# A new order for a three-layer kernel: gap memsets as operations of their own, gate loads charged more, late loads searched together

## The chip, the core and the metric

The kernel runs on one core of a Trainium2 chip. The core has a matrix engine (PE, with its weight loads shown apart as PEld), a vector engine (DVE), an activation engine (ACT), a general engine (POOL) and an engine that only issues transfers (SP); sixteen DMA engines move data between DRAM and the core's SBUF. The metric is the device time of one execution in microseconds, lower is better.

## What is computed

Windowed attention (64 keys back, 4 batches, 8 heads, 576 positions), then a gated two-matrix layer with a token shift, then a layer in which a five-tap convolution gates a product before the last one:

```python
scores = q @ k.T / sqrt(64); scores = where(0 <= i - j < 64, scores, -1e9)
x = softmax(scores) @ v                               # (4, 576, 512)
xk = mu_k * x + (1 - mu_k) * x_prev; xr = mu_r * x + (1 - mu_r) * x_prev
x = sigmoid(xr @ w_r) * (relu(xk @ w_k) ** 2 @ w_v)   # 512 -> 1024 -> 512
gate = sigmoid(sum(conv_w[k] * xpad[:, k:k + S, :] for k in range(5)))
out = (gate * (x @ w_val)) @ w_out
```

Everything is float32. Products are kept near that precision by splitting each operand into a rounded high part and a low rest and adding three products (high by high, high by low, low by high).

## The kernel before

**Stages.** The 2304 positions (4 batches of S = 576 in a row) go through attention and the first layer in five blocks t of 256, 512, 512, 512 and 512 positions. Attention works in 20 units of one block and one pair of heads. `qk` computes scores, `top`, `exp`, `eps`, `rec` and `norm` are the softmax, `tr` transposes the weights, `pv` is the product with the values, `x` puts the result in place; `ldqk` and `ldv` load a unit. The first layer has products `r`, `h` and `v` (PE, line 724, 512 columns each; line 748 for block 0), whose inputs are mixed by `a` and `xm` and split by `xhi` and `xlo`. Its weights come in as `w_r`, `w_k` and `w_v` in pieces (`ld`), which DVE and ACT turn from 64-bit to 32-bit floats. Block t's result goes to a DRAM buffer x2d (`st t m`, shown as x2d<-sgs).

The second layer works by batch b. `ldx b` loads the batch from x2d into a tile xb (1152 KB, line 868; xb<-x2d). `xsum`, `xhi_` and `xlo_` make its operands, in seven pieces by Strassen's scheme. Each of the seven products `val b m1` to `m7` is 12 matmuls of 288 columns (line 1006). They share two PSUM banks, u and v. Bank u's running sum is copied off by `valu` (ACT, early<-val), and `valc` (DVE, lines 1047 and 1052) adds up and empties a bank before the next product may start in it. `gv` multiplies by the gate, `gsum`, `ghi_` and `glo_` make operands again, and `out b m1` to `m7` are the last products with copies `outu` (ACT, ou<-out). For the first three batches `o` copies a part of the output to st and `os` stores it; then `oa` on POOL adds the rest from the same ou buffers into DRAM by an accumulating transfer (out_t<-ou). An ou buffer is free again when that has landed. Batch 3 takes plain products, `out 3`.

**Gate.** For batches 0 to 2 the convolution is done early, while PE is on the first layer, in six tasks n: `cld n` loads half a batch from x2d (576 KB, line 924), `ctap n f k` are ten taps (the first on ACT, four on DVE at line 937, for two halves f), `cgate n` the sigmoid (ACT, line 941), `cst n` the store to a DRAM buffer gd (576 KB, gd<-early). `cld n` waits for the taps of n - 1, and the first tap of n for `cst n-1`. `ldg b` brings the gate back (gate<-gd). Batch 3's gate is computed late (`tap`, `part`, `acc`).

**Second weights.** They are turned and stored to DRAM during the first layer, and come back when its matrices are no longer needed: `wv2` (wk<-w_val, 1792 KB, two) and `wo2` (wr<-w_out and wol<-w_out, 1024 KB, four). The first product with them, `out 0 m1`, waits for all four `wo2`.

**Order.** Nothing is scheduled while the kernel runs. A table SLOT gives each operation of each kind a place in one overall order, and with a letter the engine where there is a choice (v DVE, a ACT, p POOL). `Plan.run` walks that order and emits each operation, so every engine, and SP's queue of transfers, executes its own operations in the table's order and waits at each for what it needs. The durations and the `moves` in the calls of `op` serve the search that made the table; besides, `run` uses them to place a few filler matmuls on PE in the first 15 us. Two operations emit more than their own engine's instruction: `ldx` has a POOL memset of the four-column gap ahead of its transfer (line 867, batch 3 only), `cld 0` one on line 923. At the start, `first` (POOL) zeroes a column of xT; `cap` makes a mask: a DVE memset (line 337), then four POOL selects; `eye` and `low` on DVE turn it and an identity into matmul operands for the first `qk`.

The line that the last stage hangs on most: `turn_s` frees the first layer's memory for the tiles of odd batches, so `ldx 1` can't start before the last `v` product has read its weights.

Of the kernel before, what the change touches and what calls it, by code (L numbers as in the profile page):

```python
# [27 lines left out]
NF = DM // P  # L28
# [15 lines left out]
    'first': '39',  # L44
    'warm': '4',
    'cap': '8',
    'ident': '6',
    'band': '243',
    'low': '9',
    'eye': '7',  # L50
    'table': '11',
    'ldmu': '1',
    'ldc': '430',
    'mu': '2',
    'omu': '26',
    'pg': '62',
    'wc0': '439 432 460',
    'wc': '461',
    'first_x': '27',
    'ldqk': '3 13 15 16 17 37 122 166 231 255 276 277 305 327 409 434 443 467 491 540',  # L60
    'ldv': '23 36 47 49 132 140 219 224 237 261 340 363 369 415 469 482 495 550 581 584',
    'qk': '10 14 18 30 43 72 128 183 252 264 278 314 338 389 410 435 453 490 513 542',
    'top': '12 19 24 33 52 80 133 195 272 284 304 322 350 406 427 446 477 507 525 586',
    'exp': '20 21 28 41 61 95 149 197 287 292 312 323 359 416 428 458 484 520 563 592',
    'eps': 'v29 p22 p38 p51 p97 p162 p150 p215 v288 p298 v329 p332 p380 v421 p429 p474 p492 p554 v566 p593',
    'rec': '31 34 46 63 105 171 161 228 289 300 331 342 381 422 447 476 504 555 577 601',
    'diag': 'v32 v35 v58 v66',
    'tp': '40 48 64 73',
    'pt': 'v42 a55 v67 a93',
    'pv': '44 56 78 96 156 205 234 247 302 325 361 376 400 442 483 508 530 572 588 614',  # L70
    'x': 'v53 v65 a86 a100 a180 a208 a235 a249 v313 a330 a366 a383 a403 a448 a486 a509 a536 v573 v604 a647',
    'norm': 'v111 v176 v189 a232 v293 v301 v337 a357 v382 a423 v450 a493 v514 v556 a583 v609',
    'tr': '119 192 225 242 294 318 343 375 399 433 454 499 515 557 587 612',
    'mask': '262 270 297 319 344 395 412 437 471 500 517 558',
    'edge': '265 281 303 321 346 405 426 444',
    'a': 'a60 a71 a94 a102 a54 a68 a101 a103 a211 a226 a257 a260 v368 v371 v386 v392 a455 v472 a549 a551 '
        'v594 a610 a734 v748',
    'xm': '70 81 99 112 75 88 126 117 240 245 286 267 373 374 417 394 511 489 568 565 689 686 736 749',
    'xlo': '74 82 106 115 77 98 127 146 254 259 339 271 379 391 420 404 545 528 582 569 714 743 752 817',
    'carry': '177 230 285 328 402 473 535 595',  # L80
    'r': '84 109 116 123 85 92 114 131 89 110 118 124 87 90 121 138 351 360 356 370 516 512 529 533 651 688 '
        '698 727 835 827 844 855',
    'sig': '125 136 142 143 365 387 388 413 526 531 544 576 670 711 738 744 850 856 865 870',
    'h': '141 151 145 147 152 167 154 169 174 181 185 186 172 184 194 198 280 282 299 295 310 326 315 347 '
        '449 407 440 457 481 478 485 494 608 611 605 641 643 648 678 675 778 774 772 786 792 800 816 820',
    'relu': 'a159 a164 a175 a178 a193 a200 a199 a201 a290 a296 v311 a317 a341 v345 a348 a349 a451 v452 v441 '
        'v470 v497 v498 a521 a522 v627 v639 a629 a642 a659 a669 a683 a684 a787 a794 v791 a805 v818 v819 '
        'v828 a833',
    'sbuf': '165 179 204 206',
    'slo': 'v188 a182 v212 a207 336 335 354 364 496 503 538 532 658 682 697 702 812 826 852 851',  # L90
    'v': '213 216 221 239 248 253 258 269 390 424 367 385 414 456 398 419 564 574 548 559 561 570 578 580 '
        '737 741 742 756 746 750 732 733 893 902 863 892 859 867 884 891',
    'x2': '263 275 283 273 425 401 459 438 597 560 571 599 753 777 766 745 905 899 901 897',
    'st': '333 358 377 397 436 431 519 501 598 606 615 635 776 780 810 770 969 940 983 903',
    'xhi': 'a246 a251 v316 a268 a378 a384 v418 a396 v539 a527 v579 v567 a699 v735 a747 v767',
    'cut': '227 266 372 393 488 562',
    'shi': '308 320 352 355 466 475 505 523 646 649 680 685 807 808 822 834',
    'sq': 'v309 v324 v353 v362 v468 a480 a534 v524 v655 a679 a696 a701 v809 a815 a823 a845',
    'staging': '0',
    'w_r ld': '25 45',  # L100
    'w_r g': '50 79',
    'w_r t': '57 76',
    'w_r s': '59 83',
    'w_r hi': 'v139 v91',
    'w_r lo': '148 144',
    'w_k ld': '69 104 155 135',
    'w_k g': '107 129 160 153',
    'w_k t': '108 130 158 137',
    'w_k s': '120 134 173 168',
    'w_k hi': 'v191 a214 a196 a187',  # L110
    'w_k lo': '223 229 203 222',
    'w_v ld': '157 170 218 217',
    'w_v g': '163 190 233 241',
    'w_v t': '202 210 238 250',
    'w_v s': '209 220 244 256',
    'w_v hi': 'a279 a274 v408 v306',
    'w_v lo': '334 291 411 307',
    'wide_x': '236',
    'turn': '860',
    'turn_s': '915',  # L120
    'turn_w': '880 868',
    'w_val ld': '541 585 624 662',
    'w_val room': '589 628 633 663',
    'w_val g': '603 630 634 664',
    'w_val t': '600 617 618 621 619 607 632 644 637 645 625 638 665 660 674 666 677 707 692 708',
    'w_val s': '616 631 636 676',
    'w_val hi': 'a623 v656 a690 a709',
    'w_val lo': '626 661 694 716',
    'w_val st': '640 654 667 673 693 700 715 724',
    'w_out ld': '668 687 713 760',  # L130
    'w_out room': '695 717 754 782',
    'w_out g': '703 718 755 788',
    'w_out t': '691 705 706 710 726 720 722 757 764 762 739 773 783 775 789 796 811 821 813 825',
    'w_out s': '704 721 763 806',
    'w_out hi': 'v729 v768 a802 v829',
    'w_out lo': '730 781 804 837',
    'w_out st': '758 731 769 784 803 824 831 838',
    'wv2': '890 839',
    'wo2': '917 881 896 873',
    'ldx': '861 920 952 1004',  # L140
    'gbuf': '869 925 1025 1051',
    'ldg': '871 966 1077',
    'xhi_': 'a882 v878 v876 a886 a889 a906 a933 a971 a927 a937 a953 a961 a970 a1005 a994 a1002 a1026 a1028 '
        'a1087 v1127 a1075 a1098 a1143 a1117',
    'xlo_': '898 909 883 887 911 912 934 973 932 942 974 964 988 1078 1009 1011 1056 1038 1091 1138 1093 1113 '
        '1147 1136',
    'xsum': '866 879 885 888 923 930 945 955 980 993 1022 1027 1074 1081 1103 1115',
    'val': '904 908 918 921 924 929 936 939 944 946 959 976 986 992 998 1082 1019 1035 1043 1088 1062 1107 '
        '1100 1122 1133 1142 1155 1161',
    'valu': 'a910 a919 a926 a943 a963 a977 a1014 a1039 a1053 a1110 a1126 a1149',  # L150
    'valc': '913 931 935 941 951 985 990 1001 1083 1054 1101 1073 1123 1153 1174 1168',
    'gv': '914 938 949 947 999 1000 996 1017 1092 1114 1120 1086 1152 1179 1195 1170',
    'ghi_': 'v916 a948 a962 a957 a967 a982 a987 a1006 a1032 a1049 a1018 a1031 a1040 a1042 a1094 a1102 a1144 '
        'a1128 a1139 a1157 v1148',
    'glo_': '922 956 972 958 968 997 989 1033 1044 1050 1024 1036 1045 1046 1111 1116 1145 1129 1140 1158 1151',
    'gsum': '950 960 965 978 1015 1029 1034 1041 1121 1131 1137 1146',
    'out': '928 975 979 984 995 1012 1013 1037 1052 1060 1063 1068 1095 1089 1112 1125 1154 1134 1160 1166 '
        '1173 1177 1178 1186 1187 1198 1199 1200 1205',
    'outu': 'a954 a991 a1007 a1048 a1066 a1084 v1124 a1156 a1162',
    'o': '981 1010 1030 1021 1058 1085 1104 1090 1130 1163 1176 1182 1185 1193 1201 1203 1206',  # L160
    'os': '1003 1020 1071 1023 1079 1099 1164 1108 1180 1175 1181 1183 1192 1194 1202 1204 1208',
    'oa': '1008 1047 1065 1106 1135 1141 1189 1184 1188',
    'tap': '1055 1059 1069 1057 1067 1070 1064 1076 1080 1072 1097 1105',
    'part': '1016 1061 1109 1132',
    'acc': '1096 1118 1119 1167',
    'gate': '1150 1169',
    'ghi': 'v1159 v1171 v1196 v1190',
    'glo': '1165 1172 1197 1191',
    'oh': '1207',
    'cld': '445 546 650 751 801 849',  # L170
    'ctap': '462 464 479 487 502 463 465 506 510 518 575 590 591 596 613 547 552 553 602 620 653 671 719 723 '
        '728 657 672 681 712 725 761 785 790 793 797 765 771 779 795 798 832 840 841 842 843 830 836 846 '
# [1208 lines left out]
```

## Time and profile before

| | before |
|---|---|
| median of 3 runs | 412.71 us (411.44, 412.71, 413.06) |
| the profiled execution | 411.4 us |
| its span (first to last record) | 409.4 us |
| PE busy | 402.3 us, 98% of the span |
| PEld, DVE, ACT, POOL busy | 341.0, 344.7, 252.6, 27.9 us |
| granted TensorE clock | 1.00 of full speed throughout |

The span is what the trace covers; 2.0 us of the execution lie around it. A matmul is pipelined and its end is modelled, so PE counts as busy through part of a short wait: the distance from one matmul's start to the next tells more than the busy share. "Idle before" is a gap that the trace shows on an engine, with what ended it.

### The profile page before, as it was taken

How to read it: one execution, taken by the hardware profiler on the slowest of the kernel's cores; microseconds unless marked ns; L12 is line 12 of the kernel's file. 1: busy time of each engine (PE TensorE's matmuls, PEld its weight loads, DVE VectorE, ACT ScalarE, POOL GpSimd, SP SyncE). 2: the span in 40 equal slices, each digit the busy share in tenths (PEclk: the TensorE clock that was granted, in tenths of full speed). 3: DMA queues.
4: the chain of work that ended last, by engine and by line, in shares of the span. 5: the costliest groups of instructions: out<-in, count | busy, mean ns of one | idle time of the engine just before them, and what ended most of it. 6: DMA issues, size and time to landing. Idle time of an engine off the chain costs nothing.

```text
span 409.4 us, 10877 instructions
## 1 busy us (share of the span) xinstructions
PE 402.3 (98%) x4578; PEld 341.0 (83%) x4578; DVE 344.7 (84%) x516; ACT 252.6 (62%) x603; POOL 27.9 (7%) x74
## 2 busy tenths in 40 slices
PE   8999999999999999999999999999999899999996
PEld 4788887778787787788888888888889899999996
DVE  5999999999784779959979799979397699999960
ACT  5999988748435576947747643066322386866631
POOL 2001121010000000100000000000000001122010
PEclk9999999999999999999999999999999999999999
DMA  8999554050520634151378337465999906778666
GB/s 287 413 419 356 204 174 128 2 160 0 160 85 2 207 120 149 53 195 37 119 202 298 133 141 271 179 243 198 368 430 347 381 4 202 190 170 194 115 173 146
DMA packets 24673, 78.36 MB, mean 191 GB/s; under 512 B 3376, under 2 KB 6704, under 8 KB 21808
## 3 DMA queue, kind: packets, MB, share of 16 engines
q1 hardware_dynamic: 22608, 72.64, 49.3%
q0 software_dynamic: 1872, 5.01, 7.6%
q8 instruction: 36, 0.59, 0.6%
q14 instruction: 13, 0.11, 0.1%
q10 hardware_dynamic: 144, 0.00, 0.0%
HBM read 51.80 MB, written 23.49 MB: 184 GB/s over the span
## 4 chain that ended last, share of the span: by engine, by line
PE 85%; DVE 5%; DMA 5%; issue 2%; ACT 2%; POOL 0%; SPq 0%; ACTq 0%; POOLq 0%
PE h L724 22%; PE v L724 22%; PE r L724 11%; PE sv L636 5%; PE v L748 4%; PE h L748 3%; PE sv L590 3%; PE out L1118 3%; PE out2m L1006 3%; PE val3m L1006 3%; DMA xb<-x2d 2%; PE r L748 2%; DMA out_t<-ou 2%; DVE x L903 1%; PE out1m L1006 1%
## 5 line engine op out<-in xcount | busy, mean ns | idle before, releaser
L724 PE MATMUL h<-x,wk 128*128 128x512 f32 x384 | 91.3, 394 | 0.0
L724 PEld LDWEIGHTS h<-x,wk 128*128 128x128 f32 x384 | 71.2, 188 | 15.6
L724 PE MATMUL v<-sh,wv 128*128 128x512 f32 x256 | 81.3, 393 | 0.0
L724 PEld LDWEIGHTS v<-sh,wv 128*128 128x128 f32 x256 | 48.1, 188 | 10.6
L724 PE MATMUL v<-sl,wv 128*128 128x512 f32 x128 | 49.9, 390 | 0.0
L937 DVE SCALAR_TENSOR_TENSOR early<-early,wc 128x576 f32<-128x576 f32 x48 | 38.2, 810 | 12.2 <-ACT early L935 11.9
L724 PE MATMUL r<-x,wr 128*128 128x512 f32 x192 | 45.3, 391 | 0.0
L463 ACT ACTIVATE s<-s,m 128x96 f32<-128x96 f32 x104 | 37.2, 362 | 9.9 <-DVE m L452 9.9
L724 PEld LDWEIGHTS r<-x,wr 128*128 128x128 f32 x192 | 35.8, 188 | 7.6
L724 PEld LDWEIGHTS v<-sl,wv 128*128 128x128 f32 x128 | 24.1, 188 | 4.8
L776 ACT ACTIVATE rk<-h 128x512 f32<-128x512 f32 (+1 forms) x27 | 13.9, 543 | 20.6 <-PE h L724 19.0
L636 PEld LDWEIGHTS sv<-pt,vt 32*64 32x64 f32 x1536 | 18.8, 130 | 5.6 <-issue 3.1
L684 DVE SCALAR_TENSOR_TENSOR xm<-xT,omu,xm 128x512 f32<-128x512 f32 x32 | 22.4, 746 | 1.0 <-POOL xT L690 1.0
L707 DVE TENSOR_TENSOR x<-xm,x 128x1024 fp32r<-128x1024 f32 x16 | 19.5, 1220 | 3.0 <-ACT x L704 2.9
L800 ACT ACTIVATE sh<-rk 128x1024 fp32r<-128x1024 f32 x16 | 16.7, 1058 | 6.4 <-DVE rk L778 6.3
L636 PE MATMUL sv<-pt,vt 32*64 32x32 f32 (+2 forms) x1536 | 20.6, 238 | 0.0
L806 DVE TENSOR_TENSOR sl<-rk,sh 128x1024 fp32r<-128x1024 f32 x16 | 19.3, 1221 | 0.7 <-ACT rk L804 0.6
L463 ACT ACTIVATION_READ_ACCUMULATOR s<-s,m 128x1 f32 x104 | 19.8, 191 | 0.0
L830 DVE TENSOR_TENSOR sgs<-v,sgs 128x512 f32<-128x512 f32 (+1 forms) x20 | 12.3, 629 | 8.9 <-PE v L724 8.9
L935 ACT ACTIVATE early<-early,wc 128x576 f32<-128x576 f32 x12 | 8.8, 770 | 16.1 <-DMA gd<-early 10.9
L900 ACT ACTIVATE x<-xt 128x576 fp32r<-128x576 f32 x15 | 10.2, 678 | 9.9 <-DVE xt L893 9.9
L624 DVE STREAM_TRANSPOSE pt<-s 128x768 f32<-128x768 f32 x16 | 15.5, 968 | 0.4 <-ACT s L475 0.2
(226 smaller groups left out, 823.5 us busy)
## 6 DMA issues: line engine op xcount, KB each, us to landing
qk<-qk SPq DMA_DIRECT2D x16, 544.0 KB, 4.7
vt<-vh SPq DMA_DIRECT2D x16, 384.0 KB, 4.8
xb<-x2d SPq DMA_DIRECT2D x4, 1152.0 KB, 9.0
out_t<-st SPq DMA_DIRECT2D x15, 288.0 KB, 2.9
w_out<-w SPq DMA_DIRECT2D x8, 512.0 KB, 2.8
w_val<-w SPq DMA_DIRECT2D x8, 448.0 KB, 2.7
wk<-w_val SPq DMA_DIRECT2D x2, 1792.0 KB, 13.0
early<-x2d SPq DMA_DIRECT2D x6, 576.0 KB, 5.2
```

The costliest lines, as they stand in the source:

```text
L463: ACT.activation(out=s, in_=scores()[:, 2 * c // n_s, c % (n_s // 2), :] if scores else s, func=AF.Exp, scale=D ** -0.5 if scores else 1.0 ...
L624: V.transpose(out=a["pt"][:, :m2 * KW], in_=a["s"].rearrange("p c j -> p (c j)"))
L636: PE.matmul(a["o"][heads[h], i, j0 * HW:j1 * HW], lhsT=a["v"][r, k, heads[h]], rhs=p, start=k == 0, stop=k == m + 1, skip_group_check=True)
L684: V.scalar_tensor_tensor(out=m, in0=xT[:, f, :n], scalar=omu[:, c:c + 1], in1=m, op0=ALU.mult, op1=ALU.add)
L707: lambda E: E.tensor_tensor(out=dst(1), in0=src(), in1=f32(dst(0)), op=ALU.subtract))
L724: PE.matmul(ps, lhsT=a, rhs=b[:, kt, :], start=(kt == 0 and i == 0), stop=(kt == nk - 1 and i == 2))
L748: PE.matmul(Ps[key][:, :n], lhsT=ws(kt), rhs=x()[:, kt, :], start=kt == 0, stop=kt == nk - 1)
L776: ACT.activation(out=o, in_=ps, func=AF.Relu)
L800: ACT.activation(out=Ss[t][0][:, f, :n], in_=rk(), func=AF.Square)
L806: lambda E: E.tensor_tensor(out=Ss[t][1][:, f, :n], in0=rk(), in1=f32(Ss[t][0][:, f, :n]), op=ALU.subtract))
L937: V.scalar_tensor_tensor(out=o, in0=x, scalar=c, in1=o, op0=ALU.mult, op1=ALU.add)
L1006: PE.matmul(z[bank][:, j, :HS], lhsT=lhs, rhs=rhs, start=new and kt == 0 and e == 0, stop=kt == 1 and e == 2, skip_group_check=not new)
```

## The change

Three edits in the code that describes the work, and a new table. The memset of xb's gap becomes an operation `xbuf b` (on POOL for batch 3, nothing for the others), and the one of `cld 0` an operation `zero`; both stand in the order by themselves, and the transfers wait for them as before. In the costs that the search uses, a load and a store keep their duration, `moves` of `cld` goes from 1450 to 2100 and that of `ldx 3` from 4000 to 3300. Then nearly every row of SLOT has new numbers, and some operations a new engine. The work itself is the same: the same 3138 matmuls with the fillers among them, the same 149 transfers on SP's queue. After the table, the changed kernel's line numbers are 2 to 4 higher.

```diff
 SLOT = {
-    'first': '39',
-    'cap': '8',
+    'first': '0',
+    'cap': '5',
...
-    'ldx': '861 920 952 1004',
+    'xbuf': '837 922 949 1021',
+    'ldx': '849 923 964 1031',
...
+    'zero': '375',
...
     def load(b):
-        def go():
+        gap = GAP if b not in SPLIT else 0
+
+        def buffer():
             xb = Q["own", b % 2].tile([P, NF * (GAP + S)], F32, tag="xb", name=f"xb{b}")
-            gap = GAP if b not in SPLIT else 0
             Xb[b] = xb[:, :NF * (gap + S)].rearrange("p (f t) -> p f t", f=NF)
             if gap:
                 G.memset(Xb[b][:, :, 0:gap], 0.0)
-            DMA.dma_start(out=Xb[b][:, :, gap:], in_=x2d[:, b])
...
-        op(("ldx", b), "dma", 420, [("st", i, m) for i in t for m in range(NF)] + ["turn_s" if b % 2 else "turn", *last],
-           go, moves=4000 if b not in SPLIT else 2950)
+        op(("xbuf", b), "pool" if gap else "none", 120 if gap else 0, ["turn_s" if b % 2 else "turn", *last], buffer)
+        op(("ldx", b), "dma", 420, [("xbuf", b), *[("st", i, m) for i in t for m in range(NF)]],
+           lambda: DMA.dma_start(out=Xb[b][:, :, gap:], in_=x2d[:, b]), moves=3300 if gap else 2950)
...
-        def go():
-            if n == 0:
-                G.memset(cx[:, :, :GAP], 0.0)
-            DMA.dma_start(out=cx[:, :, GAP:], in_=x2d[:, b, fs])
-        op(("cld", n), "dma", 420, [("st", t, m) for t in ts for m in (2 * p, 2 * p + 1)] + old, go, moves=1450)
+        if n == 0:
+            op("zero", "pool", 120, old, lambda: G.memset(cx[:, :, :GAP], 0.0))
+            old = ["zero"]
+        op(("cld", n), "dma", 420, [("st", t, m) for t in ts for m in (2 * p, 2 * p + 1)] + old,
+           lambda: DMA.dma_start(out=cx[:, :, GAP:], in_=x2d[:, b, fs]), moves=2100)
```

Place 1, SP's queue between the second weights' first load and the load of the third batch. wk, wol and wr are second weights, gd<-early is `cst`, early<-x2d is `cld`, gate<-gd is `ldg`, x2d<-sgs is `st`; xb_3618, xb_3804 and xb_3928 are batches 0, 1 and 2 before, xb_3552, xb_3811 and xb_3906 the same ones now. Before:

```order
L1284 DMA wk_63<-w_val_106 128x3584
L1287 DMA wol_3661<-w_out_109 128x2048
L836 DMA x2d<-sgs 128x512
L943 DMA gd<-early 128x1152
L1287 DMA wr_65<-w_out_108 128x2048
L868 DMA xb_3804<-x2d 128x2304
L836 DMA x2d<-sgs 128x512
L868 DMA xb_3928<-x2d 128x2304
```

Now:

```order
L1290 DMA wr_66<-w_out_108 128x2048
L1290 DMA wol_3609<-w_out_109 128x2048
L956 DMA gate_3666<-gd 128x2304
L1290 DMA wr_65<-w_out_108 128x2048
L946 DMA gd<-early 128x1152
L1290 DMA wol_3605<-w_out_109 128x2048
L875 DMA xb_3811<-x2d 128x2304
L838 DMA x2d<-sgs 128x512
```

The big wk loads and batch 0's load stand earlier and are no longer in this stretch; the last `st` ahead of batch 1's load is now behind it; between the last `cst` and batch 1's load there is still one weight load of 1024 KB.

Place 2, ACT where batch 1's operands begin. The names early<-val0m are `valu 0`, x<-xb is `xhi_ 1 0` of batch 1, early<-early is `cgate 5`. Before:

```order
L941 ACTIVATE early<-early 128x1152
L900 ACTIVATE x<-xt 128x576
L1018 ACTIVATE early<-val0m_3742 128x576 x3
L900 ACTIVATE x<-xt 128x576
L900 ACTIVATE x<-xb_3804 128x1152
```

Now:

```order
L944 ACTIVATE early<-early 128x1152
L1021 ACTIVATE early<-val0m_3747 128x576
L903 ACTIVATE x<-xb_3811 128x1152
L1021 ACTIVATE early<-val0m_3747 128x576
L903 ACTIVATE x<-xt 128x576 x2
```

One of the three copies `valu 0` went to DVE, and the last of them stands behind an operation that waits for batch 1's load.

Place 3, ACT in the third batch's products of the first matrix. ou<-out1m are `outu 1`, st<-out1m are `o 1`, gate_4201 and gate_4211 with line 964 or 967 are `tap 3`, and sgs or tt at line 977 or 980 are `part 3`. Before:

```order
L1018 ACTIVATE ou<-out1m_4164 128x576
L900 ACTIVATE gq<-gate_3833 128x576
L1018 ACTIVATE early<-val2m_4065 128x576
L964 ACTIVATE gate_4201<-xb_4083,wc 128x576 x2
L1086 ACTIVATE st<-out1m_4202 128x576
L977 ACTIVATE sgs<-xb_4083,wc 128x576 x2
L964 ACTIVATE gate_4201<-xb_4083,wc 128x576
L1018 ACTIVATE ou<-out1m_4164 128x576
```

Now:

```order
L903 ACTIVATE gq<-gt 128x576 x2
L1021 ACTIVATE early<-val2m_4093 128x576
L1021 ACTIVATE ou<-out1m_4174 128x576
L967 ACTIVATE gate_4211<-xb_4125,wc 128x576 x2
L980 ACTIVATE tt<-xb_4125,wc 128x576 x2
L1021 ACTIVATE ou<-out1m_4174 128x576
L1089 ACTIVATE st<-out1m_4214 128x576
```

Between the first and the second `outu 1`, which empties bank u for a product of batch 1, ACT had eight operations, five of them of batch 3's gate; now it has four, all of batch 3's gate. On PE, `out 0 m3` now runs two products earlier (ahead of `val 2 m1` and `out 0 m4`, not behind `out 0 m4`), and `out 1 m7` one product earlier (ahead of `out 1 m5`). At the start, DVE's memset of `cap` is now ahead of the two casts that wait for POOL's identity, and in the first block's loads `ldv 4` stands behind two `w_k` pieces and an `ldqk`.

## Rows read from the trace of the kernel before

**Rows 1.** Page, part 1: busy us, share of the span, instructions.
```profile
PE 402.3 (98%) x4578; PEld 341.0 (83%) x4578; DVE 344.7 (84%) x516; ACT 252.6 (62%) x603; POOL 27.9 (7%) x74
```

**Rows 2.** Busy time by stretch, by engine; then clock, DMA share, GB/s.
```profile
20.00:30.00 10.00, 10.00 (x124) 8.13 (x123) 9.96 (x18) 9.95 (x29) 0.00 (x0) 1.00 1.01 415
...
310.00:320.00 10.00, 10.00 (x71) 9.65 (x70) 5.87 (x9) 1.31 (x2) 0.00 (x0) 1.00 0.98 339
320.00:330.00 10.00, 8.75 (x64) 8.31 (x63) 8.53 (x12) 3.99 (x6) 0.00 (x0) 1.00 0.70 290
...
360.00:370.00 10.00, 9.33 (x70) 9.09 (x69) 9.32 (x14) 6.02 (x10) 2.60 (x3) 1.00 0.81 172
```

**Rows 3.** PE timeline: start us, us, instruction, [idle before, what ended it].
```profile
321.54 1.76 PE L1006 MATMUL val0m<-x,wk 128*128 128x288 f32 x12
323.71 1.86 PE L1006 MATMUL val0m<-x,wk 128*128 128x288 f32 x12 [0.41 <-DVE early L1047]
326.41 0.77 PE L1006 MATMUL val1m<-x,wk 128*128 128x288 f32 x4 [0.83 <-DVE gate L1052]
...
361.54 0.29 PE L1006 MATMUL out1m<-gq,wol 128*128 128x288 f32 x1
362.51 0.54 PE L1006 MATMUL out1m<-gq,wr 128*128 128x288 f32 x2 [0.67 <-ACT ou L1018]
```

**Rows 4.** Chain that ended last, in time: start us, us, what.
```profile
290.35 21.77 PE v L724 x96
...
312.14 9.28 DMA xb<-x2d
...
331.60 1.34 DVE gq L903 x2
...
354.42 7.30 DMA out_t<-ou
...
373.97 1.60 PE out2m L1006 x12
...
404.37 1.61 PE last L1118 x12
```

**Rows 5.** DMA issues of 308.5 to 309.3 us: size, us to landing.
```profile
wr<-w_out SPq DMA_DIRECT2D x1, 1024.0 KB, 9.7
gd<-early SPq DMA_DIRECT2D x1, 576.0 KB, 5.4
```

**Rows 6.** The same, issues of 312.1 to 312.4 us.
```profile
xb<-x2d SPq DMA_DIRECT2D x1, 1152.0 KB, 9.3
```

**Rows 7.** The same, issues of 337.9 to 338.4 us.
```profile
xb<-x2d SPq DMA_DIRECT2D x1, 1152.0 KB, 5.7
```

**Rows 8.** Timelines of DVE and ACT, 283 to 322 us.
```profile
283.81 3.26 DVE L937 SCALAR_TENSOR_TENSOR early<-early,wc 128x576 f32<-128x576 f32 x4
...
307.40 1.17 ACT L941 ACTIVATE early<-early 128x1152 f32<-128x1152 f32 x1 [2.23 <-DVE early L937]
...
321.44 0.76 DVE L893 TENSOR_TENSOR xt<-xb 128x576 f32<-128x576 f32 x1 [3.21 <-DMA xb<-x2d]
```

**Rows 9.** Timelines of ACT and POOL, 349 to 355 us.
```profile
349.07 0.65 ACT L1086 ACTIVATE st<-out0m 128x576 f32<-128x576 f32 x1 [0.60 <-PE out0m L1006]
...
354.42 0.86 POOL L1091 DMA_DIRECT2D out_t<-ou  x1 [4.85 <-DMA out_t<-st]
```

**Rows 10.** Timeline of the first 8 us.
```profile
2.12 0.17 DVE L337 MEMSET cap<- 128x128 f32 x1
...
6.57 0.42 PEld L527 LDWEIGHTS s<-early 64*64 64x64 f32 x16 [0.20 <-DMA early<-qk]
...
7.30 0.69 DVE L454 TENSOR_REDUCE first_m<-s 128x4 f32<-128x512 f32 x1 [0.20 <-PE s L527]
```

**Rows 11.** DMA issues of 22.0 to 22.5 us, then PE timeline.
```profile
x<-w_k SPq DMA_DIRECT2D x1, 1024.0 KB, 10.3
...
33.43 1.28 PE L636 MATMUL sv<-pt,vt 32*64 32x32 f32 x96
```

260 rows, old and new, of the table SLOT are left out of this document.

## Prediction

> **What bounds the kernel now.** The first view is the busy time of the engines: PE holds 402.3 of 409.4 us, 98%, and no other engine comes near in a way that could set the end (PEld overlaps PE, DVE is at 84%) [rows 1]. So only time in which PE does not run can be won or lost, and the share hides where that is. The second view, busy time by stretch at a clock of 1.00 throughout, shows it: the stretch 20 to 30 and the stretch 310 to 320 are full, 320 to 330 has 8.75 us and 360 to 370 has 9.33 [rows 2]. The third is the PE timeline. I read starts, not shown idle, because the end of a matmul is modelled: one product of twelve matmuls takes 1.60 us [rows 4], one matmul 0.13 (1.60/12). The product that starts at 321.54 should be followed at 323.14 and is followed at 323.71, 0.57 late; the next comes at 326.41, 1.10 late; and the matmul after 361.54 comes at 362.51, 0.84 late [rows 3]. That is 2.5 us in three stalls. The rest of the span outside the start and the last transfer is one matmul after the other, so an order that only shuffles work there is worth nothing.
>
> The chain that ended last says the same from the other side: last `v` product from 290.35 for 21.77 us, then 9.28 us of batch 1's load, and later 7.30 us of an accumulating store; nearly all else on it is PE [rows 4].
>
> **Batch 1's load (stalls one and two).** It may be issued when the last `v` product has read its weights, at 312.1 (290.35 + 21.77), and lands 9.3 us later [rows 4, 6]. DVE has nothing else and idles 3.21 us until 321.44 [rows 8]; then it owes `xsum`, `xlo_` and the two `valc` on which PE waits, named in [rows 3] as L1047 and L1052. Why 9.3? The third batch-sized load of this kind takes 5.7 us with the queue free [rows 7]. Here a store of 576 KB and a weight load of 1024 KB, issued at 308.5 to 309.3, land 5.4 and 9.7 us later, so at about 314 and 318.5 to 319 [rows 5], and batch 1's 1152 KB follow 2.5 to 3 us behind, about what they cost at 415 GB/s (1.18 MB/415 = 2.8 us) [rows 2]. The load was not slow, it stood in line.
>
> The new order leaves the same two transfers directly ahead of it, takes the 256 KB `st` away from the head (0.6 us at 415 GB/s), and issues batch 0's load and a 1792 KB weight load earlier, in front of a load of gate data, so the backlog is worked off sooner. The last gate store hangs on eight taps of DVE (two groups of four at 3.26 us [rows 8]) and a sigmoid of 1.17 us [rows 8]. They now start from a batch 0 that is there earlier; I put the sigmoid's end at about 307 to 307.5 instead of 308.6 (307.40 + 1.17). What then lies ahead of batch 1's load at 312.1 is the end of one 1024 KB load. The lower bound of its landing is 312.1 + 5.7 = 317.8, the upper one today's 321.4. I take **318.5**: nearer to the free queue, because the two ahead are 1.6 MB, 4 us at 415 GB/s, and have over four us from 307.5 to 312.1.
>
> What PE needs: the order of its products is the same up to `val 1 m1`, so without stalls the last two `val 0` start at 321.54 and 323.14 and `val 1 m1` at 324.74. DVE is done with batch 0's first gate product at about 318.9 (before: its last operation of that kind ends some 3.21 before 321.44, at 318.2 [rows 8]; the new order gives it one copy from ACT, 0.7). From then, or from the landing if later, it does two `xsum`, one `xlo_` of double size and the first `valc`, five single operations of 0.67 (1.34 for two [rows 4]), 3.35 us, so the bank is free at 322.3, in time for 323.14. Two more `xlo_` and the second `valc` end at 324.3, in time for 324.74. On ACT a new danger stands: one `valu` is now behind batch 1's double `xhi_`, 1.15 us by the sigmoid's 1.17 for the same size [rows 8], plus 0.65 for itself, as a copy of the same size in [rows 9]. Landing plus 1.8 must stay under 321.54. Both hold for a landing up to about 319.4. Then stalls one and two are gone: **-1.67 us** (0.57 + 1.10). At a landing of 320 some 0.6 comes back; at today's 321.4 the `valu` costs 1.7 and the second `valc` 0.4, together 2.1, more than today's 1.67 by 0.4.
>
> **The accumulating store (stall three).** `out 1 m7` waits for the copy that empties bank u, and that copy for room in the staging tile, which the accumulating store on POOL holds: issued at 354.42, 7.30 to land [rows 4, 9], so 361.7. POOL waited 4.85 us for the plain store of the same rows [rows 9], which began with ACT's copy at 349.07, straight behind PE's `out 0 m3` [rows 9]. In the new order `out 0 m3` is two products earlier (3.2 us), and 1.67 more by the stalls gone: the accumulating store lands at 361.7 - 4.9 = 356.8. `out 1 m7` itself is one product earlier: 361.67 - 1.60 - 1.67 = 358.4. The copy of 0.65 then ends at 357.5, or at 358.2 if ACT's four gate operations in front (some 0.7 each, an estimate from that copy) come last. **-0.84 us**, with a margin of only 0.2; the other end is 0.
>
> **The start.** The memset of `cap` at 2.12 [rows 10] moves ahead of two casts and the mask is ready up to half a microsecond earlier. But the scores wait for a load until 6.57, and the softmax's first reduction follows PE at 7.30 [rows 10]; both stay. 0, ends -0.5 and +0.3. **The first block's loads.** `ldv 4` goes behind two `w_k` pieces and one `ldqk`. These are 1024 KB each, 10.3 us from issue to landing for the one issued at 22.0 to 22.5 [rows 11], hence 32.3 to 32.8, and `pv 4` reads its values at 33.43 [rows 11]. 0, ends 0 and +1.0. **The memsets as operations** sit on POOL, busy 7% [rows 1], ahead of transfers that wait for other things anyway; 0, at most one small memset (0.17 as [rows 10]) if POOL were late. The new charges of the gate loads exist in the search alone: 0.
>
> **The sum.** -1.67 - 0.84 = -2.5, so 411.4 becomes 408.9. The profiled execution was 1.3 below the median of the runs (412.71); the forecast for a median is 408.9 + 1.3 = **410.2**. A difference under 0.5%, 2.1 us, can hardly be told from none here; 2.5 is just over.
>
> **Rivals.** (A) *Batch 1's load stays late.* If transfers in flight shared the engines, instead of coming one behind the other, batch 1's load would share with batch 2's load and the gate load issued behind it, 3 x 1.18 MB at 415 GB/s = 8.5 us from 312.1, so 320.6 or later. Then the first two stalls stay (up to 2.1) and only the third goes: 411.4 + 0.4 - 0.84 + 1.3 = 412.3. Against it: the two of [rows 5] land 4 us apart though issued together, and the third 2.8 behind. The Trainium skill, "DMA: Bandwidth & Descriptors", section "Queues, rings and completion order", says that completion is not first in, first out per issuing engine, since a transfer runs on up to 16 engines that finish independently; by that a landing at 320.6 is possible; the trace's landings one after the other speak for turns. The same 412.3 comes out if the backlog is not cleared by 312. (B) *The accumulating store keeps its stall*, because ACT's gate operations come last: 410.2 + 0.84 = 411.0. (C) *Slower.* All eight last taps now stand in one block behind a piece of batch 0. If they end late, the 576 and 1024 KB are issued after 312 and batch 1's load lands behind them, at 323.5 (312.1 + 5.7 + 1.6 MB at 415 GB/s, 4 us, and more). ACT is in order, so the `valu` behind `xhi_` ends at 325.3 and PE starts 3.8 late, and 0.35 at the `valc` after: 4.15 for 1.67. With the third stall gone that is 411.4 + 2.5 - 0.84 + 1.3 = 414.4. It decides from a sigmoid that ends after 312, 4.5 us later than I worked out; a landing after 321.9 is enough for a loss. (D) *Nothing changes:* the three stalls are won but the last batch, whose gate is computed late and whose order changed too, waits for that gate by as much: 412.7. In before PE does not wait there, so nothing of it shows.
>
> **How the numbers follow.** Forecast 0.48 (408.3 to 410.6: to the start's gain and 0.4 of a residue); A 0.2; B 0.15; C 0.1; D 0.07. Faster by over 0.5% is the forecast and a piece of none else, 0.48; slower by over 0.5% is C and a slip of the first block, 0.1; the rest, A, B, D, is 0.42. The range goes down to 408.3, the sum with the start's gain, and up to 412.9, past A and D, leaving out C and part of the tails.
>
> **What would show it.** Batch 1's load lands 317.8 to 319.4 and DVE's idle ahead of its first `xsum` falls from 3.21 to under 0.5; the stretch 320 to 330 is full, 10.00 of PE; no idle ahead of the products at 323 and 325; the sigmoid of the last gate store ends near 307; the accumulating store lands before 357.5 and 360 to 370 is full; the chain does not pass the load of batch 1 any more. At the start the first reduction stays at 7.3 and `pv 4` does not wait. I am wrong if the load lands after 320, if PE idles at a `valu` on ACT in 320 to 330, or if a new gap of over half a microsecond stands behind 365, where batch 3's gate is due.

## The result and the profile after

The changed kernel takes 408.6 us in the median of six runs (407.76 to 409.4), the kernel before 412.52 in six (411.44 to 414.17). The ratio is 0.990, with a 95% interval of 0.9875 to 0.9925: about 1% faster, 3.9 us by the medians. The forecast was 410.2 with a range of 408.3 to 412.9 and faster as the likeliest of the three signs; the time lies in the range, near its lower end.

The two profiled executions are nearer to each other than the medians: 411.4 and 408.8 us, spans 409.4 and 407.0, 2.4 apart. That is close to the forecast's sum (2.5). So there are two things to explain: that the sum came out, and where another 1.4 us between the medians come from.

Busy time by stretch of the kernel after (columns as in [rows 2]):

```profile
310.00:320.00 10.00, 10.00 (x70) 9.61 (x69) 7.57 (x13) 1.82 (x2) 0.00 (x0) 1.00 1.01 360
320.00:330.00 10.00, 10.00 (x77) 10.00 (x76) 9.84 (x15) 5.69 (x10) 0.00 (x0) 1.00 0.50 193
360.00:370.00 10.00, 10.00 (x77) 10.00 (x76) 10.00 (x15) 7.07 (x12) 2.12 (x3) 1.00 1.00 220
```

The stretches that had 8.75 and 9.33 us of PE [rows 2] are full. DMA issues of the kernel after, at 308.1, 308.4 and 312.4 us (size, us to landing):

```profile
gd<-early SPq DMA_DIRECT2D x1, 576.0 KB, 3.1
...
wol<-w_out SPq DMA_DIRECT2D x1, 1024.0 KB, 5.8
...
xb<-x2d SPq DMA_DIRECT2D x1, 1152.0 KB, 6.0
```

The same three took 5.4, 9.7 and 9.3 us before [rows 5, 6]. Batch 1's load lands at 312.4 + 6.0 = 318.4. Timelines of DVE, ACT and PE around it:

```profile
318.89 0.75 DVE L896 TENSOR_TENSOR xt<-xb 128x576 f32<-128x576 f32 x1
...
318.43 1.17 ACT L903 ACTIVATE x<-xb 128x1152 fp32r<-128x1152 f32 x1 [0.53 <-DMA xb<-x2d]
320.44 0.65 ACT L1021 ACTIVATE early<-val0m 128x576 f32<-128x576 f32 x1 [0.85 <-PE val0m L1009]
...
321.80 3.36 PE L1009 MATMUL val0m<-x,wk 128*128 128x288 f32 x24
325.00 2.29 PE L1009 MATMUL val1m<-x,wk 128*128 128x288 f32 x16
```

DVE's first `xsum` of batch 1 shows no idle time (3.21 us in [rows 8]), the two `val 0` products are one row of 24 matmuls, and `val 1 m1` follows 3.20 us behind their start, where [rows 3] has 4.87. On the chain that ended last, batch 1's load [rows 4] is gone:

```profile
290.61 21.76 PE v L726 x96
312.37 7.99 PE val0m L1009 x60
321.96 3.20 PE val0m L1009 x24
325.16 4.80 PE val1m L1009 x36
```

The third place, timelines of POOL, ACT and PE. The accumulating store that was issued at 354.42 [rows 9] is issued at 349.25, and neither ACT's copy nor `out 1 m7` at 358.60 waits:

```profile
349.25 0.86 POOL L1094 DMA_DIRECT2D out_t<-ou  x1 [4.51 <-DMA out_t<-st]
...
357.74 0.64 ACT L1021 ACTIVATE ou<-out1m 128x576 f32<-128x576 f32 x1
...
358.60 0.43 PE L1009 MATMUL out1m<-gq,wr 128*128 128x288 f32 x2
```

From the first `val` product to the last matmul, the kernel before takes 405.97 - 311.95 = 94.02 us, the kernel after 403.56 - 312.20 = 91.36: 2.66 won, 1.66 of it up to `val 1 m1` and 1.0 behind it. Up to that first product the profile after is 0.25 later.

### The profile page after: what moved, and what is told of

Same layout as the page of the kernel before. It is cut to its first block, busy times and chain, and to the rows that moved or that the text cites. A ratio compares the mean times of both kernels' runs of the same rounds, so it can differ in the third digit from the quotient of the medians.

```text
span 407.0 us, 10877 instructions
## 1 busy us (share of the span) xinstructions
PE 402.0 (99%) x4576; PEld 341.2 (84%) x4578; DVE 346.8 (85%) x520; ACT 252.7 (62%) x608; POOL 26.3 (6%) x72
## 4 chain that ended last, share of the span: by engine, by line
PE 98%; DVE 0%; ACT 0%; issue 0%; POOL 0%; POOLq 0%
PE v L726 22%; PE h L726 22%; PE r L726 11%; PE sv L638 5%; PE v L750 4%; PE h L750 3%; PE sv L592 3%; PE out L1121 3%; PE out2m L1009 3%; PE val3m L1009 3%; PE val2m L1009 3%; PE out1m L1009 3%; PE out0m L1009 3%; PE val1m L1009 3%; PE val0m L1009 3%; PE r L750 2%
## 5 line engine op out<-in xcount | busy, mean ns | idle before, releaser
L726 PE MATMUL h<-x,wk 128*128 128x512 f32 x384 | 90.3, 392 | 0.0
L686 DVE SCALAR_TENSOR_TENSOR xm<-xT,omu,xm 128x512 f32<-128x512 f32 x32 | 22.5, 744 | 0.3 <-POOL xT L692 0.3
L386 ACT ACTIVATE s<-raw 128x512 f32<-128x512 f32 x8 | 5.4, 676 | 19.5 <-DVE w L1276 14.1
L604 DVE SCALAR_TENSOR_TENSOR s<-sv,band 128x768 f32<-128x768 f32 x12 | 11.5, 954 | 5.0 <-PE sv L592 4.5
```

What stands on the lines that cost most here:

```text
L686: V.scalar_tensor_tensor(out=m, in0=xT[:, f, :n], scalar=omu[:, c:c + 1], in1=m, op0=ALU.mult, op1=ALU.add)
L726: PE.matmul(ps, lhsT=a, rhs=b[:, kt, :], start=(kt == 0 and i == 0), stop=(kt == nk - 1 and i == 2))
```

## Experiments

Twelve runs were made, four on each of three chips, each set against the kernel before on the same chip. Where a run is set against the changed kernel of another chip, that goes by the two ratios to the kernel before, and is as uncertain as these.

**The kernel before again** (no edit).

> The kernel before, unchanged, profiled and timed a second time. The question: the medians differ by 3.9 us, the two profiled spans by 2.4 (409.4 and 407.0). Theory (noise of the start): the profiled execution of before was a fast one of its kind, and others are longer by up to 2 us in the loads of the first 20 us, which the three stalls have no part in; then this profile has the same three stalls (2.5 us together) and any difference of span lies before 20 us. Rival (the stalls vary): batch 1's load lands later in other executions, so the first two stalls are 2 to 3 us instead of 1.67, and the change takes away more than the first profile showed.

Median 411.91 against 412.07 of the others, ratio 1.000 (0.9981 to 1.0018). Its profile has a span of 410.4, not 409.4, and the difference is at the start. PE timelines of the first 9 us: in the first execution profiled, and in this one. L521 and L527 are the scores; a block is 16 matmuls of the same form.

```profile
4.15 0.54 PE L521 MATMUL qk<-low,eye 64*128 64x256 bf16 x2 [0.30 <-DVE eye L363]
4.63 0.66 PE L527 MATMUL qk<-early 64*64 64x128 f32 x16
5.46 0.66 PE L527 MATMUL qk<-early 64*64 64x128 f32 x16
6.57 0.67 PE L527 MATMUL s<-early 64*64 64x128 f32 x16
```

```profile
4.15 0.65 PE L521 MATMUL qk<-low,eye 64*128 64x256 bf16 x2 [0.30 <-DVE eye L363]
4.75 1.15 PE L527 MATMUL qk<-early 64*64 64x128 f32 x16
6.17 1.15 PE L527 MATMUL qk<-early 64*64 64x128 f32 x16
7.60 1.15 PE L527 MATMUL s<-early 64*64 64x128 f32 x16
```

The same block takes 0.66 us in one and 1.15 in the other: TensorE is at its upper level (2.4 GHz) in the first and still at the lower one (1.2 GHz) in the second, until about 8.7 us. (Fillers of 512 columns show the two levels too: six take 2.74 us from 1.10 on in both profiles, and four take 1.04 us from 7.17 on in the first.) The softmax behind it starts 1.5 us later (first transpose of weights at 10.86 instead of 9.33), and so does all that follows: the first `val` product is at 313.57 instead of 311.95. Five of the six profiles of kernels with before's start and no edit in it are of this second kind. So the execution from which the forecast was made was of the rarer kind. The theory holds in the place (the difference lies before 20 us) but not in the cause: it expected longer loads, and the trace shows a lower clock; nor do the three stalls come to 2.5 us here, but to 1.87. The rival does not hold: the first two stalls are smaller here, not larger (0.91 us in all against 1.66, with a landing 8.5 us after the issue instead of 9.3); the third is there (0.96 at the matmul that waits).

**Two loads early, in the kernel before.** `turn`, which frees their memory, has to stand ahead of them.

```diff
-    'turn': '860',
+    'turn': '839',
-    'wv2': '890 839',
-    'ldx': '861 920 952 1004',
+    'wv2': '839 839',
+    'ldx': '839 920 952 1004',
```

> The kernel before with only two loads moved: the first half of w_val and batch 0's load stand directly behind the stores of w_out, ahead of the fifth gate load, as in the changed kernel; nothing else moves. Theory: the backlog of the queue is worked off sooner, batch 1's load lands at 318.4 to 319.5 instead of 321.4, stalls one and two shrink from 1.67 to at most 0.3 and the time falls by 1.4 to 1.7 us; the third stall stays at 0.84 or less. Rival (the place of the st and of the gate's last taps matters, not the two loads): the load lands after 320.5 and under 0.5 us is gained.

419.11 us, ratio 1.018 (1.0144 to 1.0208): 7 us slower, against both theories. In its trace the fourth gate store, issued at 290.05, is behind both loads in the queue (DMA issue, then timelines of ACT and PE, then busy time by stretch):

```profile
gd<-early SPq DMA_DIRECT2D x1, 576.0 KB, 13.7
```

```profile
303.81 1.44 ACT L935 ACTIVATE early<-early,wc 128x576 f32<-128x576 f32 x2 [13.30 <-DMA gd<-early]
305.15 1.06 ACT L818 ACTIVATE sgs<-r 128x512 f32<-128x512 f32 x2
...
299.87 0.39 PE L724 MATMUL v<-sh,wv 128*128 128x512 f32 x1
305.78 0.80 PE L724 MATMUL v<-sh,wv 128*128 128x512 f32 x1 [5.52 <-ACT sgs L818]
306.80 1.05 PE L724 MATMUL v<-sh,wv 128*128 128x512 f32 x2
...
310.29 0.63 PE L724 MATMUL v<-sh,wv 128*128 128x512 f32 x2
```

```profile
300.00:312.00 12.00, 6.48 (x21) 4.96 (x20) 6.65 (x11) 3.46 (x5) 0.00 (x0) 0.72 0.97 407
```

ACT works in order: the first tap of the last gate piece waits 13.30 us for the store, and behind it stand the two sigmoid copies of line 818 that empty the bank for PE's next product. PE stands still for 5.5 us and then works at the lower clock for four more (two matmuls of 512 columns in 1.05 us instead of 0.63; granted clock 0.72 from 300 to 312). Once past that, the first two stalls are gone in this profile too (`val 0` to `val 1` in 12.79 us, seven products and one `out` at 1.60), but PE's standing still gave the queue time to clear, so this proves nothing on the two loads.

**One load early.** Only `ldx 0` (and `turn`) as above.

> The kernel before with batch 0's load alone moved ahead of the fifth gate load. With both loads there, the fourth gate store landed 13.7 us after its issue, ACT waited 13.3 us for it in front of two sigmoid copies that empty PE's bank, PE stood for 5.5 us and then ran at half clock for 4. Theory (queue): one load of 1152 KB delays that store by 2.8 us only, to about 297.5 on the time line of the first profile; the bank is emptied at 300, just about when PE needs it: 0 to 1 us of stall there, and about 1 us less at the first two stalls, so the median is between 1 us faster and 0.5 us slower than before. Rival (any early load breaks this order): over 2 us slower.

413.54, ratio 1.003 (1.0007 to 1.0051): 1.2 us slower by the medians. The gate store lands after 8.7 us, ACT waits 8.40 for it, PE stands for 0.61 behind ACT; but batch 1's load still lands 8.9 us from its issue, and the first two stalls are 1.28 together. Half of the expectation held (the price of the delayed store), half fell: moving this load by itself does nothing for the load of batch 1, and the time lies outside both ranges that were given. The order after has more than that: its last stores of w_out are issued at 276.7 (279.5 before), the w_val load that follows at 278.9 (281.8 before), and the sigmoid copies stand ahead of the gate's taps on ACT.

Busy time by stretch, as in [rows 2], shows where the queue gains. The kernel before, then the kernel after:

```profile
276.00:280.00 4.00, 4.00 (x20) 3.30 (x19) 3.86 (x7) 3.52 (x5) 0.00 (x0) 1.00 0.00 0
...
304.00:308.00 4.00, 4.00 (x19) 3.32 (x18) 3.97 (x7) 1.28 (x2) 0.00 (x0) 1.00 0.98 419
```

```profile
276.00:280.00 4.00, 4.00 (x19) 3.32 (x18) 3.93 (x6) 1.02 (x2) 0.00 (x0) 1.00 0.74 293
...
304.00:308.00 4.00, 4.00 (x19) 3.30 (x19) 3.78 (x6) 1.11 (x1) 0.00 (x0) 1.00 0.80 337
```

Before, nothing moves from 276 to 280, because SP stands at a store of w_out that waits for DVE, and from 288 to 312 the DMA share is 1.01: the gate store and the weight load issued at 308.6 and 309.0 stand in line. After, 1.2 MB move from 276 to 280, worth 2.8 us at the 415 GB/s of [rows 2], and from 304 to 308 the DMA share falls to 0.80: the queue runs empty before the gate store is issued. With batch 0's load alone moved, that load still stands behind the late stores, nothing moves from 278 to 282, and the share from 304 to 308 is 1.05. So the earlier stores of w_out look like the cause; that is read from these traces, and no run tests it.

**The third stall alone, in the kernel before.** `out 1 m7` behind `val 2 m2`, whose bank `valc` frees one tap earlier.

```diff
-    'val': '904 908 918 921 924 929 936 939 944 946 959 976 986 992 998 1082 1019 1035 1043 1088 1062 1107 '
+    'val': '904 908 918 921 924 929 936 939 944 946 959 976 986 992 998 1079 1019 1035 1043 1088 1062 1107 '
-    'valc': '913 931 935 941 951 985 990 1001 1083 1054 1101 1073 1123 1153 1174 1168',
+    'valc': '913 931 935 941 951 985 990 1001 1083 1054 1101 1070 1123 1153 1174 1168',
-    'out': '928 975 979 984 995 1012 1013 1037 1052 1060 1063 1068 1095 1089 1112 1125 1154 1134 1160 1166 '
+    'out': '928 975 979 984 995 1012 1013 1037 1052 1060 1063 1082 1095 1089 1112 1125 1154 1134 1160 1166 '
-    'tap': '1055 1059 1069 1057 1067 1070 1064 1076 1080 1072 1097 1105',
+    'tap': '1055 1059 1069 1057 1067 1073 1064 1076 1080 1072 1097 1105',
```

> The kernel before with only the place of the third stall changed: product out 1 m7 goes behind val 2 m2, and valc of batch 2 that frees the bank for it goes ahead of one tap of DVE. The accumulating store then has 1.6 us more to land. Theory: stall three (0.84 us) is gone, nothing else changes, the time falls by 0.8. Rival: the room is taken back by the gate of batch 3 or by the bank of val 2, and the gain is under 0.3.

410.72 against 412.07, 1.35 us by the medians, but a ratio of 0.9983 (0.9963 to 1.0003): neither the theory nor the rival is settled by the time. In its profile the wait at `out 1 m7` is gone (nothing behind 352 us up to `val 3`), but from the first `val 3` product to the last 0.66 is lost in two new short waits (370.09 to 373.61 for two products of 1.60, and 19.54 for twelve). In this one profile, then, most of the stall is given back 10 us later; the order after has none of that.

**Both edits in the kernel before.**

> Both of the two edits in the kernel before: the two loads early and out 1 m7 behind val 2 m2. Theory: the sum, 2.2 to 2.5 us, which is all that the changed kernel's profile has over that of before, and as fast as it within 0.5 us. Rival: if the rest of the new order carries a part of the 3.9 us between the medians, this stays 1 to 1.5 us behind the changed kernel.

418.03, ratio 1.016 (1.0127 to 1.019), with the same wait of ACT for the gate store (12.55 us). It says no more than its two parts alone.

**The start alone, in the kernel before.** DVE's memset of `cap` ahead of the two casts.

```diff
-    'eye': '7',
-    'cap': '8',
+    'eye': '8',
+    'cap': '7',
```

> The kernel before with one edit at the start: DVE's memset of cap goes ahead of the two casts that wait for POOL's identity, as in the changed kernel. Four profiles of kernels with before's start have their first three blocks of 16 score matmuls at half clock (1.15 us each) and reach the first transpose of weights at 10.9 to 11.1; the profile that the prediction read has them at full clock (0.66 each) and reaches it at 9.3. Theory (start): the 0.3 us in which PE waits for the mask, from 3.85 to 4.15, goes; the clock is at its upper level by the third block in most executions, the first transpose comes at 9.3 to 9.8, and the median falls by 1.0 to 1.5 us. Rival (the clock rises when it likes): only the 0.3 us are won and the median falls by 0 to 0.4.

410.9 against 412.34, ratio 0.9969 (0.9953 to 0.9984), 1.3 us. Two of its 12 executions take over 411.51 us, 19 of the 29 of the kernel before beside it. PE timeline of its start:

```profile
4.12 1.15 PE L527 MATMUL qk<-early 64*64 64x128 f32 x16
5.55 0.77 PE L527 MATMUL qk<-early 64*64 64x128 f32 x16
6.48 0.66 PE L527 MATMUL s<-early 64*64 64x128 f32 x16
```

The 0.30 us of idle at 4.15 are gone and the clock rises inside the second block. The theory of the start holds, the rival (0 to 0.4) falls.

**The start taken back, in the changed kernel**, and the **changed kernel again** beside it.

```diff
-    'cap': '5',
-    'eye': '6',
+    'cap': '6',
+    'eye': '5',
```

> The changed kernel with that edit taken back: the two casts ahead of the memset of cap. Theory (start): the first three score blocks are at half clock again, and the median is 1.0 to 1.5 us above the changed kernel's, at 409.6 to 410.1. Rival: within 0.4 us of the changed kernel.

> The changed kernel unchanged, beside the others on the same chip: median 408.6, no stall of PE over 0.15 us behind 312 us, batch 1's load landing 5.9 to 6.1 us from its issue. Theory (start): the third block of scores at full clock. Rival: in some profiles the start is as in before and the span 408.5.

410.44 and 408.64 us, ratios to the kernel before 0.9946 (0.9927 to 0.9966) and 0.9908 (0.9885 to 0.9930): the one edit is worth about 0.4%, 1.6 us by the ratios and 1.8 by the medians. Ten of the twelve executions with the edit taken back take 410.0 us or more, and all six of the changed kernel under 409.3; the other two, at 408.4, are no slower than the changed kernel, as if the clock had risen early there (neither was profiled). PE timelines, with the edit taken back and with the changed kernel as it is:

```profile
4.23 0.69 PE L523 MATMUL qk<-low,eye 64*128 64x256 bf16 x2 [0.36 <-DVE eye L365]
4.87 1.15 PE L529 MATMUL qk<-early 64*64 64x128 f32 x16
6.30 1.15 PE L529 MATMUL qk<-early 64*64 64x128 f32 x16
7.73 1.15 PE L529 MATMUL s<-early 64*64 64x128 f32 x16
```

```profile
4.16 0.68 PE L529 MATMUL qk<-early 64*64 64x128 f32 x16
5.01 0.66 PE L529 MATMUL qk<-early 64*64 64x128 f32 x16
6.29 0.67 PE L529 MATMUL s<-early 64*64 64x128 f32 x16 [0.25 <-DMA early<-qk]
```

In neither profile does PE stop for over 0.15 us behind 312 us. That the kernel with before's start is still 0.54% faster than the kernel before (0.34% to 0.73%) is the part of all the rest of the change, with the late stage in it: 2.2 us by the ratio, 1.9 by the medians. So of the 3.7 us between the medians on this chip the start has 1.8 and the rest 1.9.

**A filler in the pause, in the kernel before.** One matmul that computes nothing, more than before.

```diff
-                n = self.fill(s, int((t - s - 250) // self.PASS[t > self.COLD]))
+                n = self.fill(s, int((t - s - 250) // self.PASS[t > self.COLD]) + (s < 2000))
```

> The kernel before with one more of its filler matmuls on PE in the first 4 us (0.43 us at half clock), in the gap between the last filler and the first score matmul at 4.15, which waits for the mask as before. It tells two parts of the start apart. Theory (no pause): the pause itself keeps the clock low; with the gap filled the second or third score block is at full clock (0.66 us for 16 matmuls instead of 1.15), although the mask is no earlier, and the median falls by 0.8 to 1.4 us. Rival (earlier mask): what counts is that the scores begin 0.35 us earlier; the start is as in before and the median within 0.3 us of it.

Its profile has all three blocks at full clock (0.66, 0.66, 0.66 from 4.72), though the scores start no earlier than before, and a span of 408.5. The medians are 411.18 and 412.69, 1.5 apart, but the ratio is 0.998 (0.996 to 1.0001), so the time does not settle it, though none of its twelve executions takes over 412.06 us and 21 of the 29 of the kernel before do. The trace speaks for the pause; the comparison leaves the size open between nothing and 1.6 us.

**An extra transfer ahead of batch 1's load, in the changed kernel.** One or two copies DRAM to DRAM of 1152 KB each, behind the last `wo2`.

```diff
+    spare = [dram.tile([P, 2304], F32, name=f"spare{i}") for i in range(1)]
...
+                if c and j:
+                    for i in range(1):
+                        DMA.dma_start(out=spare[i], in_=flat4(wd["w_val", i])[:, :2304])
```

> The changed kernel with one more transfer of 1152 KB (DRAM to DRAM, its result unused) in SP's queue ahead of batch 1's load. Theory (the load decides): at 415 GB/s it costs 2.8 us of the queue, of which some is hidden behind the wait for the last v product; batch 1's load lands about 1.5 us later in the stage (7.5 us from its issue instead of 6.0), on the edge of what the order bears: 0 to 0.5 us of stall at the second valc or at the valu behind the double xhi_. Median 0 to 0.6 us above the changed kernel.

> The same with two such transfers. Theory: the load lands about 10.3 us from its issue; the valu on ACT ends 1.8 us after the landing, so the product m4 of batch 0 starts about 2.5 us late, and the second valc adds 0.3: 2.5 to 3.2 us above the changed kernel, with the first of the stalls ended by ACT. Rival (the order takes late loads in its stride): under 1 us.

With one: ratio 0.9953 (0.9934 to 0.9973), 0.45% above the changed kernel's, 1.9 us, where 0 to 0.6 was expected. Batch 1's load lands 9.1 us from its issue, not 7.5: nothing of the extra transfer is hidden. What follows from the landing is as worked out (DMA issue, then ACT and PE):

```profile
xb<-x2d SPq DMA_DIRECT2D x1, 1152.0 KB, 9.1
```

```profile
320.55 1.17 ACT L904 ACTIVATE x<-xb 128x1152 fp32r<-128x1152 f32 x1 [3.61 <-DMA xb<-x2d]
321.62 0.63 ACT L1022 ACTIVATE early<-val0m 128x576 f32<-128x576 f32 x1
...
322.31 3.65 PE L1010 MATMUL val0m<-x,wk 128*128 128x288 f32 x24 [1.31 <-ACT early L1022]
```

PE waits for the `valu` that ACT does behind the double `xhi_`, 1.7 us behind the landing at 320.54; `val 0` to `val 1` takes 326.10 - 311.25 = 14.85 instead of 12.80, so 2.05 us are lost. That is the price that the forecast gave for a landing like before's (2.1), and more than the old order paid for the same landing (1.66). With two: 416.11, ratio 1.011 (1.0081 to 1.0141); the load lands 14.1 us from its issue, PE waits 6.3 us for the same copy and then works at the lower clock. The mechanism was as expected, the size was not (by the ratios some 8 us above the changed kernel, where 2.5 to 3.2 was expected), since the second copy cost 5.0 us of the queue where the first cost 3.1. Why the second costs more stays open.

**`out 0 m3` put back, in the changed kernel.**

```diff
-    'out': '932 960 963 984 990 1019 1008 1046 1063 1065 1078 1073 1094 1092 1127 1119 1145 1161 1162 1175 '
+    'out': '932 960 963 984 990 1019 1020 1046 1063 1065 1078 1073 1094 1092 1127 1119 1145 1161 1162 1175 '
-    'o': '970 1006 1026 1014 1074 1086 1123 1097 1142 1170 1180 1185 1192 1199 1205 1209 1212',
+    'o': '970 1006 1026 1022 1074 1086 1123 1097 1142 1170 1180 1185 1192 1199 1205 1209 1212',
```

> The changed kernel with product out 0 m3 put back behind out 0 m4, and its copy with it, 3.2 us later as in before. Theory (accumulating store): it is issued 3.2 us later (near 352.5 instead of 349.25 on the time line of the profile after), lands near 359.7, and out 1 m7, whose turn is at 358.6, waits until about 360.5: a stall of 1.7 to 2 us there, ended by ACT's copy, and a median as much above the changed kernel. Rival (the store of other rows ends the wait): under 0.5 us.

Ratio 0.9945 (0.9929 to 0.9961), 0.37% above the changed kernel's, 1.5 us; 1.0 by the medians. POOL, ACT and PE:

```profile
351.17 0.86 POOL L1094 DMA_DIRECT2D out_t<-ou  x1 [6.75 <-DMA out_t<-st]
...
359.21 0.65 ACT L1021 ACTIVATE ou<-out1m 128x576 f32<-128x576 f32 x1 [1.13 <-DMA out_t<-ou]
...
359.92 0.54 PE L1009 MATMUL out1m<-gq,wr 128*128 128x288 f32 x2 [0.92 <-ACT ou L1021]
```

The accumulating store is 1.9 us later (not 3.2, since the plain store before it landed sooner after its copy), takes 8.0 us, and the stall is back at the same place, by the same chain: 1.08 us there, where 1.7 to 2 was expected, and 0.35 at `out 0 m3` itself, which now waits for DVE.

## Why the prediction held, and which step of it did not

**What bounds the kernel**: right. All that was won behind 312 us was PE's idle time at the three places named, and after the change no pause is left there.

**Batch 1's load**: right in the forecast's own numbers. 318.5 was taken, 318.4 came; the sigmoid was put to end at 307 to 307.5 and the store behind it was issued at 308.1, half a microsecond later, which cost nothing; stalls one and two were put at 1.67 and 1.66 is gone in the profile. The reason given holds in half. The queue is worked off before the gate store is issued, as was said. But the sigmoid ahead of that store ends only 0.5 us earlier than before (308.06 instead of 308.57), and the two loads are not enough: moved alone, they made the kernel slower, and by the traces it is the stores of w_out in front of them that let the queue gain. The size holds for the one profile; in five others of before's order the same two stalls are 0.3 to 1.3 us, since the load lands 7.9 to 8.9 us from its issue there, so in the median rather 1 than 1.67 was to be had.

**The accumulating store**: right. 0.84 was forecast, 1.0 is gone between `val 1 m1` and the end, and putting `out 0 m3` back brings a stall back by the chain described. The landing was put at 356.8; issue 349.25 and 7.2 us to land make 356.45. ACT's copy came last, at 357.74, behind the gate operations, and was in time by 0.2, as said.

**The start**: the step that failed. It was put at 0, "ends -0.5 and +0.3", since the scores wait for a load and the softmax's reduction follows them. That is so in the one execution that was read, where TensorE was at its upper level from the first block on. In most executions it was not, and there the first 16-matmul blocks set the reduction, not the load: three blocks at 1.15 us. The edit that moves `cap` takes away the pause in which the clock stayed low, and is worth 1.3 us (in the kernel before) to 1.8 us (in the changed one).

**Profile to median**: the other half of the same error. 411.4 lay 1.3 under the median, and the forecast carried these 1.3 over to the changed kernel as if they were noise: 408.9 became 410.2. They were the price of the lower clock at the start, which the change takes away in most executions. The sum without that step, 408.9, is 0.3 from the median measured; that is partly luck, since its 2.5 us for the late stage are more than the 1.9 to 2.2 found for all but the start.

The range is luck as well. Its lower end of 408.3 is explained as the sum with the start's gain; but 0.5 taken from the forecast of 410.2 gives 409.7, and from the profile's 408.9 gives 408.4. A lower end worked out for a median, at 409.7, would have lain above the 408.6 measured. What put the time below it is the term of the start, put at 0 and at best at -0.5, and worth 1.3 to 1.8.

**Rivals.** (A), a late load, did not happen, but its price is confirmed by the extra transfer: a landing like before's costs the new order 2.05 us. (C), the slow one, has its mechanism seen in another place: in the kernel with the two loads early an in-order ACT waits for a late store in front of a copy that PE needs. Its landing at 323.5 lies 1.7 above the sum that is given for it (312.1 + 5.7 + 4 = 321.8), and no run here shows that remainder. (B) was missed by 0.2 us, (D) shows nothing.

The first block's loads, the memsets as operations and the charges were put at 0, and no wait appears at any of them.

## What to carry to other kernels

When the profiled execution lies at an edge of the runs, find out what the other executions have that this one has not, before the difference is carried over as a constant: profile the kernel before a second time. At the start of a kernel, treat a pause of a few tenths of a microsecond on PE as a question of the clock, not as its own length. And before a load is moved up in a queue, list which store or load falls behind it, which in-order engine waits for that, and what stands behind that wait.

## What the runs showed of the hardware

The clock at the start: with PE busy without a pause from 1.1 us (fillers, then scores at 3.8), the first block of 0.66 to 0.69 us starts between 4.15 and 6.95 us in the seven such profiles; with 0.30 to 0.36 us of idle ahead of the first scores, six of seven profiles are at 1.15 until about 8.7. The granted clock of those stretches is listed as 1.00 all the same, so at the start the durations tell what that column does not. The Trainium skill, "TensorE: Matmul & The Clock Gate", section "Part 1: The HAM clock gate (the "warmup" mystery)", says that the point of the rise differs between executions, since what watches the activity is not started by the kernel; these traces agree as to the difference: the changed kernel's first block of scores takes 1.15 us in one profile and 0.68 in the other.

After 5.5 us without a matmul (the two loads early), 512-column matmuls came 0.43 us apart instead of 0.23 for four microseconds: as an estimate from these figures, 1.9 us were lost so, and this stall cost about a third more than itself.

In some executions PE stops for 0.3 to 0.6 us between 46 and 48 us, with no wait for an engine or a transfer that the profile shows; what causes it stays open. It occurs in the changed kernel as in three others, but not in the two profiles compared first (PE timeline of the changed kernel, second profile):

```profile
46.38 0.45 PE L638 MATMUL sv<-pt,vt 32*64 32x64 f32 x28 [0.64 <-issue]
```
